# Attention on one core: six more pieces of TensorE work get a fixed place behind a named kind of matmul

## The chip, the cores and the metric

The kernel runs on one core of a Trainium2 chip. The metric is the device time in microseconds (us), as the median of several runs. Five engines of the core take part: TensorE (PE, with its weight loads shown apart as PEld), VectorE (DVE), ScalarE (ACT), GpSimd (POOL) and SyncE (SP), which here issues the DMAs.

## What is computed

Three stages stand behind one another: a recurrent linear attention, a feed-forward block with a convolution and a gate, and a causal attention with four heads, of which each token mixes two. The change touches the third stage alone. Cut to that stage, the reference is:

```python
def _moe2_ref(x, w_gate, wq, wk, wv, wo):          # x: 4 x 768 x 384, four heads of width 64
    logits = x @ w_gate                            # the two largest of four give each token its weights w
    for e in range(4):
        q, k, v = x @ wq[e], x @ wk[e], x @ wv[e]
        scores = (q @ k.transpose(0, 2, 1)) / 8
        scores = np.where(causal, -1000000000.0, scores)
        a = np.exp(scores - scores.max(-1, keepdims=True))
        a /= a.sum(-1, keepdims=True) + 1e-09
        out += (mask_e * w_e)[..., None] * (a @ v @ wo[e])
    return out
```

## The kernel before

The first two stages (`phase1`) have an order on every engine that is written out by hand. The attention stage (class `Attention`, method `run`) has not: its instructions are written down in one list, and the tile library's planner puts them on the engines' queues with a timeline of its own. It takes the instruction that was written first among those whose inputs and buffers it believes to be ready. What it decides is fixed when the program is built; on the chip each engine works through its queue in order, and semaphores make it wait where an input is late.

The stage works on 16 units. Unit j belongs to batch j // 4, to a pair of heads, and to the first or the second half of the 768 rows (odd units have the second half, save the last two units, which are swapped). A unit has two heads (e = 0, 1) and three blocks of 128 rows each (q = 0, 1, 2). I write "score block 5.01" for unit 5, head 0, block 1. The work of a unit:

- `soft` (lines 1076 to 1100): score block. Two matmuls, or four for rows of more than 512 keys, at line 1086: one against `sk`, one against `sl` (the keys' high and low parts). Then DVE adds the mask and takes the extreme (line 1099), and ACT the exponential (line 1100). In an odd unit block 0 has moving tiles of 512 columns, block 1 twice 320, block 2 twice 384; in an even unit they are 256, 256 and 384. By these shapes the blocks can be told in the trace. The result lies in one of two buffers of the tag `st` in PSUM.
- `transp` (lines 1108 to 1126): DVE (POOL from unit 13 on) scales the block (lines 1113, 1115), TensorE transposes it in tiles of 128 by 128 (line 1120) into one of two buffers of the tag `t`, and ACT and DVE take turns to copy them out (lines 1124, 1126).
- `av` (line 1136): the product with the values; its result is split into a high part by ACT (line 1139) and a low part by DVE (line 1140).
- `proj_out` (line 1148): the output projection of three row blocks, after the second pair of heads of a half. ACT copies it out (line 1155), SP stores it (line 1156).

Beside the units run the projections: `qk_group` (nine matmuls at line 1012 for each half of q and of k of a pair of heads) and, once in a batch, six `v_group` (nine matmuls at line 1042). A key projection is split by ACT (line 1015) and DVE (line 1016), and then SP issues eight DMAs that lay it out as `sk` (lines 1023, 1024) and `sl` (lines 1032, 1033). `av`, `proj_out`, `qk_group` and `v_group` share two PSUM buffers of the tag `m`.

`run` writes the list in steps. Step j interleaves the score blocks of unit j, the tail of unit j - 1 (its transposes, its `av`, and the output projections where they are due), and the projections for later units. One piece has a fixed place already: score block 4b+1.10 is queued behind the last projection matmul that was written (lines 1196 to 1198), with `issue_after`. That call ties the order of two instructions on TensorE's queue and adds no semaphore.

The profile's lines are those of the listing here.

Of the kernel before, what the change touches and what calls it, by code (L numbers as in the profile page):

```python
# [47 lines left out]
DIAG_ON_ACT = 6  # L48
STEPS = (2, 1, 1, 1, 1, 1, 1, 1, 1, 1, 1, 1, 1, 0)
FROM = 8  # L50


def _f(ap):
# [852 lines left out]


class Attention:
    def __init__(self, tc, nc, a, x2, out, ident):
        self.tc, self.nc, self.a, self.x2, self.out, self.ident = tc, nc, a, x2, out, ident  # L910
        self.left, self.right = ExitStack(), ExitStack()
        self.flip, self.raw = True, {}

    def open_left(self):
        tc, nc, a = self.tc, self.nc, self.a
# [85 lines left out]
    def qk_group(self, xs, hl, n, p, h):  # L1001
        nc = self.nc
        w, sc = (self.wq, -0.125) if n == "q" else (self.wk, 1.0)
        if h == 0:
            hl[n] = [self.qp.tile([128, S], F32R, name=n + z, bufs=1) for z in "hl"]
        hi, lo = hl[n]
        s = slice(h * HT, (h + 1) * HT)
        pt = self.ps_m.tile([128, 512], F32, name="m")
        m = 0
        for i in range(3):  # L1010
            for wi, xi in self.P3:
                self.shown = nc.tensor.matmul(pt[:, 0:HT], w[wi][:, i, p * 128:(p + 1) * 128], xs[xi][:, i, s],
                                              start=(m == 0), stop=(m == 8))
# [12 lines left out]
        hl["s" + n] = ts  # L1026
        if n == "k":
            hl["sl"] = []
            for j in range(2):
                o, z = slice(64 * j, 64 * j + 64), slice(64 - 64 * j, 128 - 64 * j)  # L1030
                t = self.lp.tile([128, S], F32R, name=f"sl{j}")
                nc.sync.dma_start(_f(t[o]), _f(lo[o]))
                nc.sync.dma_start(_f(t[z]), _f(lo[o]))
                hl["sl"].append(t)

    def v_group(self, xs, V, t):
# [2 lines left out]
        m = 0  # L1039
        for i in range(3):  # L1040
            for xi, wi in self.P3:
                nc.tensor.matmul(pt[:, 0:260], xs[xi][:, i, t * C:(t + 1) * C], self.wv[wi][:, i],
                                 start=(m == 0), stop=(m == 8))
                m += 1
        if t in V_ON_DVE:
            nc.vector.tensor_copy(V[:, t], pt[:, 0:260])
# [29 lines left out]
    def soft(self, hl, j, qi, A, rs):  # L1076
# [6 lines left out]
        st = self.ps_s.tile([128, 2, 512], F32, name="st")  # L1083
        for z in range(nb):
            for i, k in enumerate((hl["sk"][j], hl["sl"][j])):
                nc.tensor.matmul(st[:, z, 0:n], q[:, qi * C:(qi + 1) * C], k[:, z * n:(z + 1) * n], start=(i == 0),  # L1086
                                 stop=(i == 1))
# [20 lines left out]
    def transp(self, A, rs, T, qi):  # L1108
# [7 lines left out]
        for k0 in range(0, qi + 1, 4):  # L1116
            k1 = min(qi + 1, k0 + 4)
            pt = self.ps_t.tile([128, 4, C], F32, name="t")
            for ki in range(k0, k1):
                nc.tensor.transpose(pt[:, ki - k0], at[:, ki * C:(ki + 1) * C], self.ident)  # L1120
            self.flip = not self.flip
            to = T[:, k0:k1, q * C:(q + 1) * C]
            if self.flip:
# [4 lines left out]
    def av(self, Ts, V, p, h, O):  # L1128
# [3 lines left out]
        for ki in range(n):  # L1132
            lo = max(0, ki - 3 * h) * C
            for j in range(2):
                o = slice(64 * j, 64 * j + 64)
                nc.tensor.matmul(po[o, lo:HT], V[:, ki, (2 * p + j) * 64:(2 * p + j + 1) * 64], Ts[j][:, ki, lo:],  # L1136
                                 start=(ki == 0), stop=(ki == n - 1))
# [4 lines left out]
    def proj_out(self, b, O, t):  # L1142
# [2 lines left out]
        m = 0  # L1145
        for p in range(2):
            for oi, wi in self.P3:
                nc.tensor.matmul(pt[:, 0:DM], O[oi][:, p, t * C:(t + 1) * C], self.wo[wi][:, p], start=(m == 0),  # L1148
                                 stop=(m == 5))
# [8 lines left out]
    def run(self):  # L1158
# [26 lines left out]
        def softs(j):  # L1185
# [3 lines left out]
            for e in range(2):  # L1189
                for q in range(3):  # L1190
                    def f(e=e, q=q):
                        if q == 0:
                            A = ap.tile([128, (6, 15)[h] * C], F32, name=f"A{h}", bufs=3)
                            rs = sp.tile([128, 3], F32, name="rs", bufs=6)
                            st[j].append((A, rs))
                        if j % 4 == 1 and (e, q) == (1, 0):
                            with self.tc.issue_after(self.shown.ins):
                                self.soft(HL[i], e, 3 * h + q, *st[j][e])
                        else:
                            self.soft(HL[i], e, 3 * h + q, *st[j][e])  # L1200
                    todo.append(f)
            return todo
# [1 line left out]
        def tail(j):  # L1204
# [4 lines left out]
            for e in range(2):  # L1209
                for q in range(3):  # L1210
                    def f(e=e, q=q):
# [14 lines left out]
            if half[b, h] == 2:  # L1226
                for t in range(3):
                    todo.append(lambda t=t: self.proj_out(b, OS[b], 3 * h + t))
            return todo

        st, half = {}, {}
# [142 lines left out]
```

## Time and profile before

| | before |
|---|---|
| median of 3 runs | 597.36 us |
| the three runs | 596.36, 597.47, 597.36 us |
| the profiled execution | 596.38 us |
| its span from the first to the last instruction | 594.7 us |
| attention stage in the span | from about 358 us to the end |
| PE busy, whole span | 95% |

The profiled execution lasted 1.7 us longer than its span; this part is launch and end, and nothing of it is in the rows. The ends of matmuls are modelled: two matmuls of 384 columns show about 0.34 us each, and start 0.175 us apart in a run of them. So a busy PE is not one without stalls, and the starts are what to compare.

### The profile page before, as it was taken

How to read it: one execution, taken by the hardware profiler on the slowest of the kernel's cores; microseconds unless marked ns; L12 is line 12 of the kernel's file. 1: busy time of each engine (PE TensorE's matmuls, PEld its weight loads, DVE VectorE, ACT ScalarE, POOL GpSimd, SP SyncE). 2: the span in 40 equal slices, each digit the busy share in tenths (PEclk: the TensorE clock that was granted, in tenths of full speed). 3: DMA queues.
4: the chain of work that ended last, by engine and by line, in shares of the span. 5: the costliest groups of instructions: out<-in, count | busy, mean ns of one | idle time of the engine just before them, and what ended most of it. 6: DMA issues, size and time to landing. Idle time of an engine off the chain costs nothing. (4 is left out here: it accounts for less than half of the span.)

```text
span 594.7 us, 12388 instructions
## 1 busy us (share of the span) xinstructions
PE 563.1 (95%) x4386; PEld 507.1 (85%) x4386; DVE 493.5 (83%) x1153; ACT 398.0 (67%) x1015; POOL 173.3 (29%) x246
## 2 busy tenths in 40 slices
PE   4788989999999999999999999999999999999986
PEld 4676888999999999989999999697979788978754
DVE  6999999999999999999967774988768667884741
ACT  4986657767778788887775765765666565654632
POOL 3666562335344342425310000400030021002440
PEclk9868889999999999999999999999999999999999
DMA  7676524664747868775453326760376153606202
GB/s 238 229 254 197 176 78 132 200 171 127 215 131 212 289 226 257 236 219 181 121 161 99 120 57 168 215 156 6 107 213 146 38 122 96 159 27 152 63 1 86
DMA packets 47158, 90.41 MB, mean 152 GB/s; under 512 B 14320, under 2 KB 28656, under 8 KB 47088
## 3 DMA queue, kind: packets, MB, share of 16 engines
q1 hardware_dynamic: 47088, 89.53, 51.2%
q8 instruction: 37, 0.61, 0.4%
q14 instruction: 33, 0.27, 0.2%
HBM read 50.23 MB, written 9.44 MB: 100 GB/s over the span
## 5 line engine op out<-in xcount | busy, mean ns | idle before, releaser
L447 PE MATMUL hs<-X,win 128*128 128x384 f32 (+1 forms) x576 | 118.1, 349 | 1.0 <-ACT ht L451 1.0
L447 PEld LDWEIGHTS hs<-X,win 128*128 128x128 f32 x576 | 98.9, 189 | 3.9 <-ACT ht L451 1.7
L521 PE MATMUL x<-gh,wout 128*128 128x386 f32 (+1 forms) x384 | 100.3, 343 | 0.0
L1099 DVE CUSTOM_DVE_ANT_0 sm<-st,mask 128x128 f32<-128x128 f32 (+5 forms) x96 | 58.6, 618 | 26.7 <-PE st L1086 23.4
L484 ACT ACTIVATE st<-ct 128x382 f32<-128x382 f32 (+1 forms) x64 | 33.7, 527 | 68.7 <-DVE ct L479 35.4
L1100 ACT ACTIVATE A<-sm,mn 128x128 f32<-128x128 f32 (+5 forms) x96 | 63.7, 664 | 20.1 <-DVE mn L1099 19.1
L302 POOL TENSOR_SCALAR_AFFINE_SELECT AT<-e 128x384 f32<-128x384 f32 x52 | 43.6, 859 | 108.9 <-DVE e L292 107.7
L521 PEld LDWEIGHTS x<-gh,wout 128*128 128x128 f32 x384 | 71.7, 193 | 0.0
L521 PE MATMUL x<-gl,wout 128*128 128x382 f32 (+1 forms) x192 | 65.8, 343 | 0.0
L1120 PE MATMUL t<-ident,A 128*128 128x128 f32 x336 | 51.7, 275 | 1.9 <-ACT T L1124 0.8
L1120 PEld LDWEIGHTS t<-ident,A 128*128 128x128 f32 x336 | 39.8, 140 | 8.0 <-issue 2.6
L1086 PE MATMUL st<-sk,sq 128*128 128x384 f32 (+3 forms) x128 | 44.2, 352 | 0.9 <-DVE mn L1099 0.6
L1136 PE MATMUL m<-T,V 128*64 128x384 f32 (+2 forms) x288 | 44.2, 422 | 0.3 <-ACT T L1124 0.3
L1086 PE MATMUL st<-sl,sq 128*128 128x384 f32 (+3 forms) x128 | 41.0, 328 | 2.8 <-DMA sl<-kl 2.8
L1126 DVE COPY T<-t 128x128 f32<-128x128 f32 (+3 forms) x64 | 32.2, 503 | 13.0 <-PE t L1120 12.2
L493 DVE SCALAR_TENSOR_TENSOR st<-st,ht 128x382 f32<-128x382 f32 (+1 forms) x64 | 36.4, 568 | 7.1 <-ACT st L484 5.4
L258 DVE TENSOR_TENSOR_SCAN Dp<-wkr,cD 128x387 f32<-128x387 f32 x32 | 39.1, 1221 | 3.6 <-POOL cD L174 3.6
L455 ACT ACTIVATE ct<-ht,cwk 128x382 f32<-128x382 f32 (+1 forms) x64 | 39.5, 618 | 2.1
L1124 ACT ACTIVATE T<-t 128x512 f32<-128x512 f32 (+3 forms) x64 | 28.5, 446 | 17.3 <-PE t L1120 17.0
L310 ACT ACTIVATE Fp<-wkr,lim 128x384 f32<-128x384 f32 x64 | 38.8, 607 | 0.3
L1136 PEld LDWEIGHTS m<-T,V 128*64 128x64 f32 x288 | 20.8, 136 | 20.0 <-issue 14.4
L319 PE MATMUL sc<-Q,K 64*128 64x128 f32 x384 | 35.2, 314 | 2.2 <-DVE AT L325 2.2
(148 smaller groups left out, 1313.8 us busy)
## 6 DMA issues: line engine op xcount, KB each, us to landing
wkr<-in_wkr SPq DMA_DIRECT2D x25, 578.0 KB, 4.1
v<-in_rkv SPq DMA_DIRECT2D x32, 192.0 KB, 3.9
rawt<-in_win SPq DMA_DIRECT2D x8, 768.0 KB, 5.6
rawt<-in_wout SPq DMA_DIRECT2D x8, 768.0 KB, 5.6
sk<-kh SPq DMA_DIRECT2D x32, 192.0 KB, 3.4
sl<-kl SPq DMA_DIRECT2D x32, 192.0 KB, 4.0
rn<-in_rkv SPq DMA_DIRECT2D x20, 288.0 KB, 3.6
x<-x SPq DMA_DIRECT2D x12, 384.0 KB, 4.5
```

The lines of the kernel that those rows point to most:

```text
L258: nc.vector.tensor_tensor_scan(fl(t["Dp"]), t["w"][:, 0:NW], fl(cD), 0.0, op0=OP.mult, op1=OP.add)
L302: nc.gpsimd.affine_select(AT[:, j], t["e"][:, j][:, :, None].to_broadcast([128, CH, C]), pattern=[[0, CH], [1, C]], compare_op=OP.is_equal ...
L310: nc.scalar.activation(Fp[:, :, 0:C], wc, AF.Relu, bias=lim[:, z:z + 1], scale=(-1.0, 1.0)[z], accum_out=stat[:, 2 * u + z:2 * u + z + 1])
L447: nc.tensor.matmul(hs[:, 0:N], win[wi][:, f // 2, i, (f % 2) * 128:(f % 2 + 1) * 128], x[:, i, xi], start=(n == 0), stop=(n == 8))
L455: nc.scalar.activation(ct, ht[:, o:o + N], AF.Copy, scale=w[:, 1, f:f + 1])
L493: nc.vector.scalar_tensor_tensor(st, st, 1.0, ht[:, o:o + N], op0=OP.add, op1=OP.mult)
L521: nc.tensor.matmul(acc[0][i][:, 0:N], wout[wi][:, f, i * 128:(i + 1) * 128], G[g][gi], start=(f == 0 and z == 0), stop=(f == NF - 1 and z ...
L1086: nc.tensor.matmul(st[:, z, 0:n], q[:, qi * C:(qi + 1) * C], k[:, z * n:(z + 1) * n], start=(i == 0), stop=(i == 1))
L1099: nc.vector.tensor_tensor_reduce(o3, i3, m3, 1.0, 3e38, op0=OP.add, op1=OP.min, accum_out=mn)
L1100: nc.scalar.activation(at, o3, AF.Exp, bias=mn, scale=-1.0, accum_out=rs[:, qi % 3:qi % 3 + 1])
L1120: nc.tensor.transpose(pt[:, ki - k0], at[:, ki * C:(ki + 1) * C], self.ident)
L1136: nc.tensor.matmul(po[o, lo:HT], V[:, ki, (2 * p + j) * 64:(2 * p + j + 1) * 64], Ts[j][:, ki, lo:], start=(ki == 0), stop=(ki == n - 1))
```

## The change

A table `PINS` names seven pieces by (unit number modulo 4, kind, head, block) and for each a kind of matmul. While the list is written, the kernel keeps the last matmul of each kind (`last`). A named piece is then written inside `issue_after` of the last matmul of its kind, so that all its TensorE instructions are queued behind that one. The first entry is the tie that was there before. The ties hold in the program's main path alone (`fast`); the other path, which runs only when an input lies out of range, has none now. No instruction is added, removed or altered.

In words: of units 0, 4, 8, 12, score block .01 comes behind the last score matmul written, and .02 behind the last value projection; of units 1, 5, 9, 13, score block .01 comes behind the last transpose written (that is block .01 of the unit before), .10 behind the last q or k projection (as before), transposes .11 behind the last `av`, transposes .12 behind the last output projection; of units 2, 6, 10, 14, transposes .11 come behind the last value projection.

```diff
+PINS = {(1, "st", 1, 0): "qk", (2, "t", 1, 1): "v", (1, "t", 1, 2): "o", (1, "t", 1, 1): "av", (1, "st", 0, 1): "t", (0, "st", 0, 2): "v",
+        (0, "st", 0, 1): "st"}
...
+    def behind(self, j, what, e=0, q=0):
+        p = PINS.get((j % 4, what, e, q))
+        if self.fast and p in self.last:
+            return self.tc.issue_after(self.last[p].ins)
+        return ExitStack()
...
-                self.shown = nc.tensor.matmul(pt[:, 0:HT], w[wi][:, i, p * 128:(p + 1) * 128], xs[xi][:, i, s],
+                self.last["qk"] = nc.tensor.matmul(pt[:, 0:HT], w[wi][:, i, p * 128:(p + 1) * 128], xs[xi][:, i, s],
...
-                        if j % 4 == 1 and (e, q) == (1, 0):
-                            with self.tc.issue_after(self.shown.ins):
-                                self.soft(HL[i], e, 3 * h + q, *st[j][e])
-                        else:
+                        with self.behind(j, "st", e, q):
                             self.soft(HL[i], e, 3 * h + q, *st[j][e])
...
-                        self.transp(A, rs, Ts[e], 3 * h + q)
+                        with self.behind(j, "t", e, q):
+                            self.transp(A, rs, Ts[e], 3 * h + q)
...
-                self.av(Ts, VS[b], p, h, OS[b])
+                with self.behind(j, "av"):
+                    self.av(Ts, VS[b], p, h, OS[b])
...
+                def out(t):
+                    with self.behind(j, "o", 0, t):
+                        self.proj_out(b, OS[b], 3 * h + t)
...
-    at = Attention(tc, nc, a, x2, out, ident)
+    at = Attention(tc, nc, a, x2, out, ident, True)
```

## Rows read from the trace of the kernel before

**Rows 1.** The page, part 1 (busy time of engines) and the clock line of part 2.
```profile
PE 563.1 (95%) x4386; PEld 507.1 (85%) x4386; DVE 493.5 (83%) x1153; ACT 398.0 (67%) x1015; POOL 173.3 (29%) x246
...
PEclk9868889999999999999999999999999999999999
```

**Rows 2.** Waits of PE, 355 to 595 us: total us, times, longest us.
```profile
PE st L1086 <- DMA sl<-kl: 2.8, 4, 1.0
```

**Rows 3.** PE timeline around units 5 and 6: start, us, instruction, idle before it.
```profile
409.24 0.42 PE L1086 MATMUL st<-sk,sq 128*128 128x384 f32 x1
...
415.96 0.31 PE L1086 MATMUL st<-sk,sq 128*128 128x320 f32 x1
...
416.55 0.60 PE L1120 MATMUL t<-ident,A 128*128 128x128 f32 x4
...
418.22 0.34 PE L1086 MATMUL st<-sk,sq 128*128 128x384 f32 x1
...
418.92 0.81 PE L1120 MATMUL t<-ident,A 128*128 128x128 f32 x6
...
420.63 1.73 PE L1012 MATMUL m<-xs,wq 128*128 128x384 f32 x9
...
426.54 0.49 PE L1120 MATMUL t<-ident,A 128*128 128x128 f32 x3
...
428.45 0.39 PE L1086 MATMUL st<-sk,sq 128*128 128x512 f32 x1
...
434.88 0.36 PE L1086 MATMUL st<-sk,sq 128*128 128x256 f32 x1
...
436.63 0.35 PE L1086 MATMUL st<-sl,sq 128*128 128x256 f32 x1 [0.70 <-DMA sl<-kl]
```

**Rows 4.** PE timeline, the same places of units 8 to 10 and 13 to 14.
```profile
461.28 0.48 PE L1086 MATMUL st<-sl,sq 128*128 128x256 f32 x2 [0.45 <-DMA sl<-kl]
...
477.88 0.32 PE L1086 MATMUL st<-sk,sq 128*128 128x320 f32 x1
...
493.40 0.36 PE L1086 MATMUL st<-sl,sq 128*128 128x256 f32 x1 [1.05 <-DMA sl<-kl]
...
529.97 0.31 PE L1086 MATMUL st<-sk,sq 128*128 128x320 f32 x1
...
551.11 0.48 PE L1086 MATMUL st<-sl,sq 128*128 128x512 f32 x1 [0.60 <-DMA sl<-kl]
```

**Rows 5.** Timeline of SP: the DMAs that lay out unit 6's keys.
```profile
429.17 0.46 SPq L1023 DMA_DIRECT2D sk<-kh  x1
...
432.43 0.89 SPq L1033 DMA_DIRECT2D sl<-kl  x1
```

**Rows 6.** Busy time by stretch: us, then PE, PEld, DVE, ACT, POOL (instructions), clock, DMA.
```profile
404.88:420.63 15.75, 15.75 (x107) 12.12 (x105) 13.64 (x59) 9.98 (x30) 0.20 (x1) 1.00 0.06 23
...
428.45:436.63 8.18, 7.48 (x51) 5.15 (x50) 4.24 (x10) 5.87 (x12) 6.28 (x9) 1.00 0.90 209
...
485.07:493.40 8.33, 7.28 (x49) 4.93 (x48) 4.88 (x12) 6.16 (x13) 6.27 (x9) 1.00 0.94 225
...
542.92:551.11 8.19, 7.59 (x50) 5.20 (x50) 4.32 (x10) 3.37 (x8) 0.00 (x0) 1.00 0.89 209
561.00:578.00 17.00, 15.21 (x97) 9.62 (x97) 10.67 (x32) 8.26 (x24) 9.43 (x11) 1.00 0.01 1
```

**Rows 7.** ACT timeline: what frees an m buffer for the next output projection.
```profile
417.68 0.49 ACT L1155 ACTIVATE ot<-m 128x384 f32<-128x384 f32 x1
```

**Rows 8.** Groups by shape, 357 to 595 us: exponentials and masks of the longer blocks.
```profile
L1099 DVE CUSTOM_DVE_ANT_0 sm<-st,mask 128x768 f32<-128x768 f32 x16 | 15.2, 952 | 3.7 <-PE st L1086 3.3 <-ACT A L1100 0.2
L1100 ACT ACTIVATE A<-sm,mn 128x768 f32<-128x768 f32 x16 | 14.9, 930 | 2.2 <-DVE mn L1099 2.2
L1100 ACT ACTIVATE A<-sm,mn 128x640 f32<-128x640 f32 x16 | 13.2, 827 | 4.4 <-DVE mn L1099 4.4
L1099 DVE CUSTOM_DVE_ANT_0 sm<-st,mask 128x640 f32<-128x640 f32 x16 | 13.0, 814 | 2.0 <-PE st L1086 1.9
```

More of the change, by code (lines that the diff above doesn't have):

```diff
@@ L908, with __init__ @@
 class Attention:
-    def __init__(self, tc, nc, a, x2, out, ident):
+    def __init__(self, tc, nc, a, x2, out, ident, fast=False):
+        self.fast = fast
         self.tc, self.nc, self.a, self.x2, self.out, self.ident = tc, nc, a, x2, out, ident
         self.left, self.right = ExitStack(), ExitStack()
-        self.flip, self.raw = True, {}
+        self.flip, self.raw, self.last = True, {}, {}
+    def behind(self, j, what, e=0, q=0):
[3 more added lines that the diff above has]
+        return ExitStack()
     def open_left(self):
@@ L1011, in qk_group @@
             for wi, xi in self.P3:
-                self.shown = nc.tensor.matmul(pt[:, 0:HT], w[wi][:, i, p * 128:(p + 1) * 128], xs[xi][:, i, s],
-                                              start=(m == 0), stop=(m == 8))
+                self.last["qk"] = nc.tensor.matmul(pt[:, 0:HT], w[wi][:, i, p * 128:(p + 1) * 128], xs[xi][:, i, s],
+                                                   start=(m == 0), stop=(m == 8))
                 m += 1
@@ L1041, in v_group @@
             for xi, wi in self.P3:
-                nc.tensor.matmul(pt[:, 0:260], xs[xi][:, i, t * C:(t + 1) * C], self.wv[wi][:, i],
-                                 start=(m == 0), stop=(m == 8))
+                self.last["v"] = nc.tensor.matmul(pt[:, 0:260], xs[xi][:, i, t * C:(t + 1) * C], self.wv[wi][:, i],
+                                                  start=(m == 0), stop=(m == 8))
                 m += 1
@@ L1085, in soft @@
             for i, k in enumerate((hl["sk"][j], hl["sl"][j])):
-                nc.tensor.matmul(st[:, z, 0:n], q[:, qi * C:(qi + 1) * C], k[:, z * n:(z + 1) * n], start=(i == 0),
-                                 stop=(i == 1))
+                self.last["st"] = nc.tensor.matmul(st[:, z, 0:n], q[:, qi * C:(qi + 1) * C],
+                                                   k[:, z * n:(z + 1) * n], start=(i == 0), stop=(i == 1))
         w = W // nb
@@ L1119, in transp @@
             for ki in range(k0, k1):
-                nc.tensor.transpose(pt[:, ki - k0], at[:, ki * C:(ki + 1) * C], self.ident)
+                self.last["t"] = nc.tensor.transpose(pt[:, ki - k0], at[:, ki * C:(ki + 1) * C], self.ident)
             self.flip = not self.flip
@@ L1135, in av @@
                 o = slice(64 * j, 64 * j + 64)
-                nc.tensor.matmul(po[o, lo:HT], V[:, ki, (2 * p + j) * 64:(2 * p + j + 1) * 64], Ts[j][:, ki, lo:],
-                                 start=(ki == 0), stop=(ki == n - 1))
+                self.last["av"] = nc.tensor.matmul(po[o, lo:HT], V[:, ki, (2 * p + j) * 64:(2 * p + j + 1) * 64],
+                                                   Ts[j][:, ki, lo:], start=(ki == 0), stop=(ki == n - 1))
         s = slice(h * HT, (h + 1) * HT)
@@ L1147, in proj_out @@
             for oi, wi in self.P3:
-                nc.tensor.matmul(pt[:, 0:DM], O[oi][:, p, t * C:(t + 1) * C], self.wo[wi][:, p], start=(m == 0),
-                                 stop=(m == 5))
+                self.last["o"] = nc.tensor.matmul(pt[:, 0:DM], O[oi][:, p, t * C:(t + 1) * C], self.wo[wi][:, p],
+                                                  start=(m == 0), stop=(m == 5))
                 m += 1
@@ L1226, in tail @@
             if half[b, h] == 2:
+                def out(t):
+                    with self.behind(j, "o", 0, t):
+                        self.proj_out(b, OS[b], 3 * h + t)
                 for t in range(3):
-                    todo.append(lambda t=t: self.proj_out(b, OS[b], 3 * h + t))
+                    todo.append(lambda t=t: out(t))
             return todo
```

## The prediction

> **What bounds the kernel now.** I read the page first. TensorE is busy for 95% of the span, and from the third of forty slices on its clock is granted in full [rows 1]. No instruction is added or taken away, so the time can change only by what TensorE waits. The waits of TensorE in the attention stage come next: 2.8 us in four places go to score matmuls whose `sl` has not landed [rows 2], and no other releaser comes near this. The reader should see that this is nearly all that a better order can bring back in the middle of the stage. The TensorE timeline then tells where: at the first score block of units 6, 8, 10 and 14 [rows 3, 4]. In each the high-part matmul has been issued, and the low-part matmul stands at the head of the queue with everything else behind it. The waits shown are 0.70, 0.45, 1.05 and 0.60 us. The modelled end of the matmul before hides another 0.17 us of each (0.345 us shown against 0.175 us from start to start), so that the real losses are 0.87, 0.62, 1.22 and 0.77 us.
>
> Why the keys are late can be read from SP's timeline. Unit 6's key projection ends at 428.45 us, where the next kind of matmul starts [rows 3]. SP then issues four DMAs for `sk` from 429.17 us, and the second for `sl` of head 0 from 432.43 us to 433.32 us [rows 5]; the matmul that needs it starts at 436.63 us [rows 3]. So 8.18 us pass from the projection to the first use, and of these TensorE had other work queued for 8.18 - 0.87 = 7.31 us. The planner counted on an earlier landing; the chip doesn't give it.
>
> **The change part by part.** First, which ties bind at all. Read against the order of before, most hold already. Score block 4.02 stands behind the last value projection of its batch, transposes 5.11 stand behind `av`, and 5.12 behind the output projections; the same is so in the other batches. These I cost at nothing: they only keep what is there, and could bind only if the rest moves much. Score block .01 behind block .00 shifts one matmul at unit 8, which stood in front of the same `sl` wait: nothing, as the wait takes it up. Transposes 6.11, five matmuls with 6.12, go behind the last value projection; they feed an `av` that comes later in any case: nothing, at most their 0.3 us. The tie of .10 is the old one.
>
> One tie binds hard: score block .01 of units 5, 9 and 13 behind transposes .01 of the unit before. In unit 5 the block starts at 415.96 us, and the tie's target at 426.54 us [rows 3]. So the block, 0.59 us from start to start (415.96 to 416.55 us), must go back by some 10 us, past the second half of the output projections and past the next q projections. Units 9 and 13 have theirs at 477.88 and 529.97 us, just as early [rows 4].
>
> Does block .02 go with it? I take it that it does. At 409.24 us TensorE took score block 4.02, while the q projection that starts at 420.63 us had been written earlier and lacked nothing but an `m` buffer [rows 3]; `av` and output projections that were written before it had to be served first. So I read that the planner hands out a tag's buffers in written order, and then block 5.02 can't have an `st` buffer before 5.01. It is 0.70 us (418.22 to 418.92 us) [rows 3]. Together 1.29 us of TensorE work leave the time ahead of the key projection and come back behind it; the other way, 0.59 us alone, is a rival below.
>
> What it brings. The projections of q and k come up to 1.29 us earlier, and so does every DMA behind them, and the work between the key projection and the first score block of unit 6 grows from 7.31 us to 8.60 us, over the 8.18 us that the keys take. The waits of 0.87, 1.22 and 0.77 us before units 6, 10 and 14 are then covered: 2.86 us. The wait of 0.62 us at unit 8 has another projection ahead of it and stays.
>
> What it costs. The two vacated places, 0.59 and 0.70 us, have to be filled by what stood behind them. If nothing were ready, TensorE would idle for all of it, 3 times 1.29 us = 3.87 us; if all were ready, nothing. At 416.55 us four transposes follow; at the second place the next output projection needs an `m` buffer which ACT empties from 417.68 to 418.17 us [rows 7], and TensorE would be there some 0.6 us before 418.22 us [rows 3]. On the other side DVE, with 13.64 of 15.75 us busy [rows 6], loses two mask passes of 0.814 and 0.952 us [rows 8] in just this stretch, so that what it feeds to TensorE is ready earlier. I take 0.2 us for each batch, 0.6 us in all, near the lower end, since the row puts the buffer within 0.6 us.
>
> Behind the key projection the two blocks bring DVE 1.77 us and ACT 1.76 us [rows 8]. DVE has room: 4.24 of 8.18, 4.88 of 8.33 and 4.32 of 8.19 us are busy there [rows 6]. ACT has less: 5.87 + 1.76 = 7.63 of 8.18 us, 6.16 + 1.76 = 7.92 of 8.33 us, and 3.37 + 1.76 = 5.13 of 8.19 us. Who waits for ACT there: the copies of transposes and the high part of `av`, which output projections read. I cost this at nothing, and keep it as a rival. The transposes of unit 5 need all three blocks of head 0; they come after 436.63 us, with some 6 us to spare, and cost nothing.
>
> The sum: -2.86 + 0.6 = -2.26 us. On the profiled execution of 596.38 us (span 594.7 us) that gives 594.1 us. That execution lies 0.98 us under the median of the runs; from the median of 597.36 us it is **595.1 us**.
>
> **The rivals.** *Only the tied block moves, or the planner uses the gain up.* If 5.02 overtakes 5.01, only 0.59 us move, and the waits fall to 0.28, 0.63 and 0.18 us at best: 1.77 us gained. But the planner puts the `sl` matmul where its own timeline has the keys landed. Where that is right beside the `sk` matmul, the added cover goes to work behind it and nothing is gained. Half of 1.77 us less 0.3 us for one vacated place is -0.6 us: 596.8 us. For it speaks that ties are single and the planner free; against it, the served order of the `m` buffers.
>
> *ACT becomes the bound behind the key projections.* In two of three stretches it would be 93% and 95% busy by the sums above; an exponential in front of a transposes' copy or of `av`'s high part holds TensorE, which works in order. If all 1.76 us come through in both, and the third stretch alone gains, it is 597.36 + 3.52 - 0.77 + 0.6 = 600.7 us. It decides from the point where the high part of the `av` in that stretch leaves ACT more than 0.9 to 1.2 us later after its last matmul than now, which is what the covered wait brings. Against it: the exponentials may slip past 436.63 us, as transposes 5.00 need them only then.
>
> *The clock.* With the scores gone, the places before 420.63 us are denser in transposes and short waits. The granted clock is 1.00 in all these stretches, and also from 561 to 578 us, where TensorE works through transposes with 1.8 us idle [rows 6]. If it fell to its lower level (1.2 in place of 2.4 GHz), the 4.67 - 1.29 = 3.4 us from 415.96 to 420.63 us would double in three batches: about 607.5 us. The Trainium skill ("TensorE: Matmul & The Clock Gate", section "Part 4: PE-mode transpose") states that the full clock does not engage for the transpose mode, because it does not count as busy in the same way; it speaks against denser transposes. By that rule the clock should have dropped near the end of this trace already, and the row does not agree.
>
> **How the numbers follow.** Forecast: 0.50, with a range of its own from 593.9 us (2.86 and 0.62 us regained, no cost) to 596.1 us (1.0 us less gain). First rival 0.30, about 595.9 to 598.4 us. ACT 0.19, from 598.6 to 601 us. Clock 0.01. A difference under about 0.2%, 1.2 us, can't be told from no change; so faster 0.50, same 0.30, slower 0.20. The runs of before alone spread by 1.1 us, so I let the range begin 1.0 us under the forecast's own, at 592.9 us, and end at 599.6 us, inside the ACT case; about 0.15 is left out.
>
> **What would show it.** In the profile after, score blocks 5.01 and 5.02 (320 and 384 columns) stand behind the key projection; the q projection follows the output projections at once; the waits for `sl` at units 6, 10 and 14 are gone and that at unit 8 is left, about 0.5 us of the 2.8 us. Wrong if the waits are still there with the blocks moved (then the planner used the gain up), if waits on ACT or on DVE take their place, or if the granted clock leaves 1.00. It would also be wrong if the blocks' move upset the order far behind it, in the last 30 us, where TensorE waits on short chains anyway; that I can't price.

## The result and the profile after

The changed kernel takes 591.38 us in the median (590.90 to 591.97), the kernel before 597.41 us beside it: a ratio of 0.9900, 95% interval 0.9889 to 0.9910, or 6.0 us less. The forecast was 2.26 us less, 595.1 us, with a range from 592.9 to 599.6 us: the sign was right, but the gain is 2.6 times the forecast's, and the time lies 1.5 us under the range.

The page of the kernel after, part 1 and the clock line of part 2 (beside [rows 1]):

```profile
PE 560.0 (95%) x4386; PEld 506.0 (86%) x4386; DVE 497.9 (84%) x1153; ACT 398.5 (68%) x1015; POOL 174.7 (30%) x246
...
PEclk9879798999999999999999999999999999999999
```

The waits of PE after, 355 to 595 us: who waits, for whom, total us, times, longest us.

```profile
PE t L1129 <- ACT T L1133: 1.0, 2, 0.6
PE st L1095 <- DVE mn L1108: 0.9, 3, 0.4
PE t L1129 <- DVE T L1135: 0.5, 1, 0.5
```

The line for `sl` [rows 2] is gone, with all its four waits, that of unit 8 among them.

To see where the time went, I look for points at which both kernels have issued the same set of matmuls. The time from the first value projection of the attention stage to such a point can be compared directly, whatever stands in between. Here are seven such points in the PE timeline of before (start, us, instruction), and between 525 and 529 us the `av` of unit 10, which comes up further down.

```profile
357.86 0.28 PE L1042 MATMUL m<-wv,xs 128*128 128x260 f32 x1
...
403.72 0.37 PE L1042 MATMUL m<-wv,xs 128*128 128x260 f32 x1
...
426.79 0.42 PE L1012 MATMUL m<-xs,wk 128*128 128x384 f32 x1
...
471.14 0.33 PE L1148 MATMUL m<-wo,O 128*128 128x384 f32 x1
...
525.04 0.86 PE L1136 MATMUL m<-T,V 128*64 128x384 f32 x2
525.83 0.39 PE L1086 MATMUL st<-sk,sq 128*128 128x256 f32 x1
...
527.04 1.51 PE L1136 MATMUL m<-T,V 128*64 128x384 f32 x10
528.48 0.33 PE L1120 MATMUL t<-ident,A 128*128 128x128 f32 x1
...
541.25 0.42 PE L1012 MATMUL m<-xs,wk 128*128 128x384 f32 x1
...
554.12 0.34 PE L1148 MATMUL m<-wo,O 128*128 128x384 f32 x1
...
587.50 0.68 PE L1148 MATMUL m<-wo,O 128*128 128x384 f32 x3
```

And the PE timeline of after: the same points, and between 425.37 and 437.76 us the moved blocks and the neighbourhood of unit 6's keys.

```profile
359.12 0.28 PE L1051 MATMUL m<-wv,xs 128*128 128x260 f32 x1
...
403.74 0.28 PE L1051 MATMUL m<-wv,xs 128*128 128x260 f32 x1
...
425.37 0.40 PE L1095 MATMUL st<-sk,sq 128*128 128x320 f32 x1
...
426.05 0.34 PE L1095 MATMUL st<-sk,sq 128*128 128x384 f32 x1
...
426.75 1.75 PE L1021 MATMUL m<-xs,wk 128*128 128x384 f32 x9
428.34 0.60 PE L1129 MATMUL t<-ident,A 128*128 128x128 f32 x4
...
432.25 0.50 PE L1095 MATMUL st<-sk,sq 128*128 128x512 f32 x1
...
437.56 0.36 PE L1095 MATMUL st<-sk,sq 128*128 128x256 f32 x1
437.76 0.28 PE L1095 MATMUL st<-sl,sq 128*128 128x256 f32 x1
...
469.04 0.34 PE L1157 MATMUL m<-wo,O 128*128 128x384 f32 x1
...
536.83 0.34 PE L1021 MATMUL m<-xs,wk 128*128 128x384 f32 x1
...
548.78 0.34 PE L1157 MATMUL m<-wo,O 128*128 128x384 f32 x1
...
582.55 0.68 PE L1157 MATMUL m<-wo,O 128*128 128x384 f32 x3
```

| point | us after the first value projection, before | after | difference |
|---|---|---|---|
| last value projection of the second batch (403.72, 403.74) | 45.86 | 44.62 | -1.24 |
| second half of unit 6's key projection (426.79, 426.75) | 68.93 | 67.63 | -1.30 |
| first output projection of the second batch (471.14, 469.04) | 113.28 | 109.92 | -3.36 |
| second half of unit 14's key projection (541.25, 536.83) | 183.39 | 177.71 | -5.68 |
| last output projection of the third batch (554.12, 548.78) | 196.26 | 189.66 | -6.60 |
| near the end (587.50, 582.55) | 229.64 | 223.43 | -6.21 |

The stage ahead of attention, which is in the same order in both, ran 1.26 us longer in the execution of after (359.12 against 357.86 us), so that the spans, 594.7 and 589.8 us, show only 4.9 us.

Between these points I reckon finer: from the time that has passed I take off the TensorE work done by then, each matmul at its shortest start-to-start time for its shape, and compare the remainders. The 6.21 us are then: 1.3 to 1.4 us in the first units of the stage, up to 390 us; 0.92 us at unit 6, 0.69 us at unit 8, 1.28 us at unit 10 and 0.83 us at unit 14, each at its first score block; 0.3 us around the `av` of units 5 and 6; 1.2 us from the `av` of unit 9 to the first output projections of the third batch; and the last 30 us give 0.38 us back. Forecast were the terms at units 6, 10 and 14 alone, and a cost of 0.6 us.

The waits do not hold all of it. Here is the busy time from the first value projection to the end of the stage, first in before, then in after (columns as in [rows 6]):

```profile
357.86:588.90 231.04, 225.23 (x1493) 190.92 (x1492) 162.63 (x547) 137.23 (x355) 37.82 (x49) 1.00 0.42 110
```

```profile
359.12:583.95 224.83, 222.09 (x1493) 190.24 (x1492) 166.63 (x547) 136.49 (x355) 39.55 (x49) 1.00 0.43 113
```

Of the 6.21 us, 3.07 us are idle time of TensorE (5.81 us in before, 2.74 us in after). The other 3.14 us come out of its busy time, with the same matmuls: they follow each other at shorter distances.

Last, busy time by stretch in after: us, then PE, PEld, DVE, ACT, POOL (instructions), clock, DMA. The first is that of the vacated places, the second and third lie from the key projection to the first use of its keys at units 6 and 10, the fourth near the end (beside [rows 6]).

```profile
404.88:419.22 14.34, 14.34 (x97) 10.81 (x96) 11.84 (x54) 9.73 (x28) 0.20 (x1) 1.00 0.04 15
428.34:437.76 9.42, 9.42 (x65) 7.37 (x64) 7.80 (x17) 7.57 (x17) 7.06 (x9) 1.00 0.78 176
483.37:492.79 9.42, 9.42 (x65) 7.37 (x64) 7.78 (x17) 7.58 (x17) 7.05 (x9) 1.00 0.75 173
...
556.00:573.00 17.00, 14.97 (x95) 9.31 (x95) 12.07 (x35) 8.36 (x26) 10.82 (x12) 1.00 0.01 2
```

TensorE is busy without a gap in the first three, and the clock is granted in full in all.

### The profile page after: what moved, and what is told of

The parts are those of the page before. It is cut to its first block, busy times and chain, and to the rows that moved or that the text cites. A ratio compares the mean times of both kernels' runs of the same rounds, so it can differ in the third digit from the quotient of the medians.

```text
span 589.8 us, 12381 instructions
## 1 busy us (share of the span) xinstructions
PE 560.0 (95%) x4386; PEld 506.0 (86%) x4386; DVE 497.9 (84%) x1153; ACT 398.5 (68%) x1015; POOL 174.7 (30%) x246
## 4 chain that ended last, share of the span: by engine, by line
PE 72%; DVE 15%; ACT 6%; DMA 3%; issue 2%; SPq 1%; POOL 0%; ACTq 0%; DVEq 0%; POOLq 0%
PE hs L449 13%; PE x L523 13%; PE m L1021 8%; PE st L1095 7%; PE m L1145 6%; PE t L1129 6%; PE m L1157 4%; PE m L1051 4%; PE sc L321 3%; PE m L399 2%; PE m L407 2%; DVE Dp L260 2%; DVE Fp L268 1%; PE m L354 1%; DVE ct L468 1%
## 5 line engine op out<-in xcount | busy, mean ns | idle before, releaser
L449 PE MATMUL hs<-X,win 128*128 128x384 f32 (+1 forms) x576 | 120.1, 354 | 0.5 <-ACT ht L453 0.5
L449 PEld LDWEIGHTS hs<-X,win 128*128 128x128 f32 x576 | 101.0, 192 | 3.2 <-ACT ht L453 1.1
L1095 PE MATMUL st<-sk,sq 128*128 128x384 f32 (+3 forms) x128 | 45.5, 360 | 0.9 <-DVE mn L1108 0.9
L1145 PE MATMUL m<-T,V 128*64 128x384 f32 (+2 forms) x288 | 42.9, 421 | 0.0
L453 ACT ACTIVATE ht<-hs 128x384 f32<-128x384 f32 (+1 forms) x64 | 30.9, 484 | 11.5 <-PE hs L449 11.4
L510 DVE TENSOR_TENSOR gl<-st,gh 128x382 fp32r<-128x382 f32 (+1 forms) x64 | 36.2, 565 | 1.8 <-ACT gh L502 1.6
```

Source lines behind the costliest of these rows:

```text
L449: nc.tensor.matmul(hs[:, 0:N], win[wi][:, f // 2, i, (f % 2) * 128:(f % 2 + 1) * 128], x[:, i, xi], start=(n == 0), stop=(n == 8))
L1095: self.last["st"] = nc.tensor.matmul(st[:, z, 0:n], q[:, qi * C:(qi + 1) * C], k[:, z * n:(z + 1) * n], start=(i == 0), stop=(i == 1))
L1145: self.last["av"] = nc.tensor.matmul(po[o, lo:HT], V[:, ki, (2 * p + j) * 64:(2 * p + j + 1) * 64], Ts[j][:, ki, lo:], start=(ki == 0), st ...
```

## The experiments

All medians, beside runs of the kernel before on the same chip (597.06 to 597.41 us). The runs took place on several chips, so two of them are compared by their ratios to before rather than by their medians. "By the traces" means the reckoning above, from one execution of each kernel.

| run | us | ratio to before | 95% interval |
|---|---|---|---|
| the change | 591.38 | 0.9900 | 0.9889 to 0.9910 |
| a_only | 596.85 | 0.9988 | 0.9972 to 1.0004 |
| c_only | 593.45 | 0.9930 | 0.9916 to 0.9944 |
| a_and_c | 591.25 | 0.9897 | 0.9882 to 0.9911 |
| keys_early | 596.07 | 0.9973 | 0.9961 to 0.9984 |
| keys_early_after | 590.69 | 0.9886 | 0.9863 to 0.9908 |
| sl_late | 592.97 | 0.9935 | 0.9910 to 0.9961 |
| no_tie_unit0 | 592.15 | 0.9914 | 0.9891 to 0.9937 |
| whole_av | 596.53 | one run | |
| av_head1_first | 597.60 | 1.0010 | 0.9995 to 1.0026 |
| av_head1_after | 594.42 | 0.9955 | 0.9934 to 0.9975 |
| av_keys_after | 593.86 | 0.9948 | 0.9922 to 0.9973 |
| av_head1_tail | 589.89 | 0.9883 | 0.9858 to 0.9907 |

**Which ties carry it.** The lines that differ from the change are those of the table of ties. First a_only:

```diff
+PINS = {(1, "st", 1, 0): "qk", (0, "st", 0, 1): "st"}
```

> The kernel before with one tie alone, score block .01 of units 0, 4, 8 and 12 behind block .00 of the same unit (beside the old tie of .10). It changes TensorE's order in units 0 to 4 and one matmul at unit 8. Theory now: the start of the attention stage holds a gain of its own that the prediction put at nothing, 1.4 us by the comparison of the two traces; so 596.0 us beside 597.4 us, a ratio near 0.998, and the four waits for sl stay at 2.8 us. The prediction's reading (the tie is worth nothing): 597.4 us, ratio 1.000 within 0.001.

Measured: 0.5 us less, inside the interval of no change. By the traces the first units gain 1.4 us as expected, but 0.6 us of it is lost again by unit 10, 0.8 us being left at the end. The waits for `sl` took 0.13 us of that at unit 8 and 0.24 us at unit 10:

```profile
PE st L1094 <- DMA sl<-kl: 3.0, 4, 1.3
```

(waits of PE in a_only, 355 to 595 us; in before they were 2.8 us and 1.0 us at the longest [rows 2]).

Then c_only:

```diff
+PINS = {(1, "st", 1, 0): "qk", (1, "st", 0, 1): "t"}
```

> The kernel before with the other binding tie alone, score block .01 of units 1, 5, 9 and 13 behind transposes .01 of the unit before. Theory now: the move of 1.29 us of score blocks behind the key projection takes all four waits for sl, that of unit 8 with them (2.86 + 0.6 us), the vacated places cost nothing, and a value product that is no longer cut in two by transposes brings some 0.8 to 1.2 us: 4.5 us in all, 592.9 us, ratio 0.9925. The prediction's reading: unit 8 keeps its wait and the vacated places cost 0.6 us, so 595.1 us, ratio 0.996. If the tie of block .01 to .00 were behind everything: 597.4 us.

Measured: 3.9 us less, between the two and nearer to the first; by the traces 4.35 us. No wait for `sl` is left. The PE timeline of c_only at unit 8, where the prediction let the wait stand:

```profile
459.65 0.36 PE L1094 MATMUL st<-sk,sq 128*128 128x256 f32 x1
459.85 1.24 PE L1050 MATMUL m<-wv,xs 128*128 128x260 f32 x9
460.93 0.32 PE L1094 MATMUL st<-sl,sq 128*128 128x256 f32 x1
```

Between high and low part stands a value projection, and no idle time. And a_and_c:

```diff
+PINS = {(1, "st", 1, 0): "qk", (1, "st", 0, 1): "t", (0, "st", 0, 1): "st"}
```

> The two binding ties together, without the other four new ones. Theory now: they are all of the change, and they add up, 1.4 + 4.5 us: 591.5 us, ratio 0.990, as the full change. Rival: the ties behind the value projections (transposes .11 of units 2, 6, 10, 14 and block .02 of units 0, 4, 8, 12) carry part of it, and this kernel is 0.8 us or more slower than the full change: 592.3 us or more, ratio 0.9915 or more.

Measured: 591.25 us, the change's time. So two of the six new ties carry what can be measured. The traces differ by 0.77 us in the stage (5.43 against 6.21 us less), of which 0.29 us each at the `av` of units 6 and 10: with the ties to the value projections these follow the `av` before them at once, without them two transposes come in between. The times don't show that.

**Is it the landing of the keys?** In keys_early SP issues `sl` of head 0 ahead of `sk` of head 1; nothing else is changed in the kernel before:

```diff
-        hl["s" + n] = ts
-        if n == "k":
-            hl["sl"] = []
-            for j in range(2):
-                o, z = slice(64 * j, 64 * j + 64), slice(64 - 64 * j, 128 - 64 * j)
+            if n == "k":
                 t = self.lp.tile([128, S], F32R, name=f"sl{j}")
...
-                hl["sl"].append(t)
+                hl.setdefault("sl", []).append(t)
+        hl["s" + n] = ts
```

> The kernel before, with one thing changed: the DMAs that write sl of head 0 are issued by SP before those of sk of head 1, no longer behind all four of sk. No score block moves in unit 5; the planner itself puts the first score matmul of unit 6 a little earlier. Cover theory (the low-part matmul waits for a DMA that is late, whatever stands in unit 5): sl of head 0 lands about one DMA issue earlier, 0.7 us, at four units, and up to 2.6 us of the 3.5 us of waits go: 595 us, ratio 0.996. Rival (the planner spends the gain by placing the score matmul earlier by as much): waits stay at 2.8 us, 597.4 us, ratio 1.000. Under the rival, cover alone, without a change in what is queued, brings nothing.

Measured: 1.3 us less. By the traces 0.95 us are won at unit 6, 1.15 us at unit 10 and 0.95 us at unit 14; 0.14 us are lost at unit 8 and about 1.1 us in the new order behind unit 13. One wait is left in place of four. Waits of PE in keys_early:

```profile
PE t L1117 <- ACT T L1121: 1.6, 3, 0.6
PE st L1083 <- DMA sl<-kl: 0.7, 1, 0.7
```

Both theories have their part: at unit 6 the planner put the low-part matmul ahead of two matmuls (0.35 us) that stood ahead of it before, and the rest was gained; at unit 8 it put it ahead of a whole value projection that had covered part of the landing, and the wait stayed (the 0.7 us above). The same edit on the changed kernel:

> The changed kernel with sl of head 0 issued by SP ahead of sk of head 1, the edit that took 1.3 us off the kernel before. TensorE's order is the same as in the changed kernel. Cover theory: in the changed kernel the low-part matmuls of units 6, 10 and 14 start 9.4 to 9.5 us after the key projection and wait for nothing, so that a landing that is 1.3 us earlier is worth nothing: 591.4 us, within 0.8 us. Rival (the keys still set when the scores run, by a wait that the trace puts down to something else): 590.1 us, as much gain as in the kernel before.

Measured: 590.69 us, not to be told from the change's 591.38 us by the intervals; by the traces 0.13 us less in the whole stage. What brought time before brings none once the keys are covered. The other way, sl_late, in the changed kernel:

```diff
-            for j in range(2):
+            self.pairs += 1
+            late = self.pairs in (4, 6, 8)
+            for j in ((1, 0) if late else (0, 1)):
...
-                hl["sl"].append(t)
+                hl["sl"].insert(j if len(hl["sl"]) else 0, t)
```

> The changed kernel with sl of head 0 issued by SP behind sl of head 1, for the keys of units 6, 10 and 14 alone; TensorE's order is unchanged. The second DMA of sl of head 0 then starts some 1.57 us later (434.33 in place of 432.76 us for unit 6). Cover theory with the numbers of the trace after: the keys need 8.18 us and 0.44 us that SP begins later than in the kernel before, 8.62 us, and have 9.42 us; with 1.57 us more they need 10.2 us, so each of three units waits 0.8 us again and the waits for sl are back at three places: 591.4 + 2.3 = 593.7 us. With the prediction's 8.18 us: 0.33 us each, 592.4 us. Rival (the cover is far larger than the keys need, or the gain at these units was no matter of cover): no wait for sl, 591.4 us.

Measured: 592.97 us, 1.6 us more than the change by the medians and 2.1 us by the ratios; by the traces 2.30 us more, 0.84, 0.78 and 0.69 us at units 6, 10 and 14, and nothing anywhere else. PE timeline of sl_late at these units:

```profile
436.70 0.36 PE L1097 MATMUL st<-sl,sq 128*128 128x256 f32 x1 [0.59 <-DMA sl<-kl]
...
492.56 0.36 PE L1097 MATMUL st<-sl,sq 128*128 128x256 f32 x1 [0.54 <-DMA sl<-kl]
...
548.43 0.47 PE L1097 MATMUL st<-sl,sq 128*128 128x512 f32 x1 [0.46 <-DMA sl<-kl]
```

The waits are back, with TensorE's order unchanged. So the gain at these units is cover, and it is limited: the second DMA for `sl` of head 0 started 6.35 us after the key projection at unit 6 in place of 4.42 us, 1.93 us later rather than the 1.57 us I had counted, and 0.8 us of that came through. That the wait has the size expected is luck in part: the DMA came 0.36 us later than counted, but the keys also needed less than the 8.62 us counted, about 8.3 us (9.42 + 0.84 - 1.93). The changed kernel has some 1.1 us to spare.

**The start.** no_tie_unit0 is the change without one of its ties in one unit:

```diff
         p = PINS.get((j % 4, what, e, q))
+        if p == "st" and not j:
+            p = None
```

> The changed kernel without the tie of score block .01 behind block .00 in unit 0 alone; units 4, 8 and 12 keep it. The order of the first units of the attention stage is then that of the kernel before. Theory: the start's gain of 1.3 to 1.5 us hangs on this one tie, by way of the planner's order in units 0 to 4: 591.4 + 1.4 = 592.8 us. Prediction's reading (the tie is worth nothing): 591.4 us.

Measured: 592.15 us, 0.8 us more than the change, with intervals that overlap; by the traces 1.29 us more, 1.1 us of it by 404 us. The times alone don't settle it. The traces do, as far as one execution of each can: against before, the five with its start order lie at 0 to -0.15 us behind the first units, the six with the other at -1.2 to -1.4 us. What the tie does is indirect. It shifts one matmul in unit 0, and the planner, from there on, puts the transposes of unit 0 ahead of score blocks of units 1 and 2. From 375 to 404 us VectorE was busy for 26.97 of 29.00 us before and for 25.00 us of the 27.50 us from 376.5 to 404 us after; TensorE's idle time there fell from 1.22 to 0.68 us. The rest of the 1.4 us lies in matmuls that follow each other at longer distances, which the waits don't name; this stays open.

**The cut products.** In before, the `av` of unit 10 is cut behind its first matmul (525.04 and 527.04 us in the PE timeline of before above; a matmul shows as two records there); in after it is whole. From start to start the two parts are 0.79 + 1.44 = 2.23 us. A first try at it, whole_av, replaced the seven ties:

```diff
+PINS = {(1, "st", 1, 0): "qk", (2, "av", 0, 0): "t"}
```

> The kernel before with a tie of its own instead of the seven: the value product of units 2, 6, 10 and 14 stands behind the last transposes of its unit. Against the kernel before only two places change: in unit 2 the product's first matmul goes behind transposes 2.12 (it is still cut by score block 4.11), and in unit 14 it goes behind transposes 14.11 and 14.12, so that it is cut no more by transposes. Theory (a value product that other kinds of matmul cut in two costs about 0.8 us): nothing at unit 2, about 0.8 us gained at unit 14, less what the transposes' chain then waits, 596.6 us. Rival (the cut is free; the time follows the chain of transposes): 597.4 us or more.

Measured: 596.53 us in one run; by the traces nothing at unit 2 and 0.5 us less at unit 14. The number fits, but proves nothing: the product of unit 14 was still cut, by output projections now, and took 0.79 + 3.38 us as before. The gain came from the transposes that were no longer kept apart: between 571 and 575.96 us in before they wait 0.20, 0.46 and 0.56 us for other engines, in whole_av 0.20, 0.31 and 0.24 us. So av_head1_first, an edit of the product itself in the kernel before:

```diff
-            for j in range(2):
+            for j in (1, 0):
                 o = slice(64 * j, 64 * j + 64)
```

> The kernel before with one thing changed: in the value product the matmul of head 1 is written ahead of that of head 0 at each step, so that the first matmul already waits for the last copied transposes and the planner no longer issues one matmul early and the others later. The products of units 0, 2, 10 and 14 are then whole, that of unit 13 is cut after eight matmuls and not after one and nine. TensorE's order changes in many more places. Theory (a product cut behind its first matmul takes 0.78 us more: 0.79 and 1.44 us in place of 1.45 us): five such products, 3.9 us, 593.2 us; what of it falls where TensorE waits for VectorE anyway (units 0, 13, 14) is lost, so at least units 2 and 10, 1.6 us, 595.5 us. Rival (the cut costs nothing, since other work is done in between): 597.1 us. The waits for sl stay.

Measured: no gain, 597.60 us. PE timeline of av_head1_first, at the start of the stage and at unit 10 (the brackets: idle time before it, and for whom):

```profile
378.01 0.38 PE L1086 MATMUL st<-sk,sq 128*128 128x320 f32 x1 [1.06 <-DVE mn L1099]
...
528.86 1.52 PE L1136 MATMUL m<-T,V 128*64 128x384 f32 x12
530.31 0.66 PE L1120 MATMUL t<-ident,A 128*128 128x128 f32 x4
```

The price of the cut was right: the product of unit 10 takes 1.45 us from start to start, and all sixteen together went from 42.68 to 38.85 us, 3.83 us less. By the traces 1.0 us of that arrives, at unit 10. But the order of the first units changed too, with TensorE idle for 1.06 us for VectorE in one place; there, at 378 us, the kernel was 0.86 us behind, and at 394 us it was 2.2 us behind. In between the granted clock fell to its lower level (0.50, 1.2 in place of 2.4 GHz). Busy time of TensorE by stretch (us, busy, clock, DMA), in before and then in av_head1_first:

```profile
376.00:379.00 3.00, 2.75 (x14) 1.00 1.00 248
```

```profile
376.00:379.00 3.00, 1.66 (x7) 1.00 0.97 233
379.50:385.50 6.00, 5.48 (x21) 0.50 0.98 290
```

In before the clock is 1.00 in both stretches. So this run does not show that the whole products are worth nothing elsewhere: the edit's new order left TensorE idle for 1.34 of 3.00 us, the clock fell behind that, and 1.35 us of the loss came up between 378 and 394 us, waits for VectorE among it.

The same edit on the changed kernel did worse:

> The changed kernel with the same edit of the value product. In the changed kernel the product of unit 10 is already whole; those of units 0, 2, 13 and 14 are cut. Theory: between 0.8 us (unit 2 alone) and 3.1 us (all four) less than the changed kernel's 591.4 us, so 588.3 to 590.6 us; the waits for sl stay gone, since the seven ties are kept. Rival (the cut costs nothing): 591.4 us, or more where the new order brings waits.

Measured: 594.42 us, 3.0 us more than the change; by the traces 4.26 us more: 3.5 us lost up to 389 us and 1.4 us more around 438 us, where an output projection waits for VectorE, and 1.1 us won in the last 30 us. Of the 3.5 us, 0.58 us are lost by 378 us and the other 3.0 us from there to 389 us, where the clock was at 0.50 again (in after it is 1.00):

```profile
379.50:385.50 6.00, 5.35 (x18) 0.50 0.91 277
```

With the earlier `sl` beside it:

> The kernel of the run before this one, and sl of head 0 issued ahead of sk of head 1; TensorE's order is the same as in that run. Cover theory: with the ties in place the earlier landing is worth nothing where no wait for sl is left, so the time of that run, 588.3 to 590.6 us; it would be up to 0.8 us less if the new order had left a wait for sl at one unit.

Measured: 593.86 us, not to be told from the run before it. By the traces it is 0.79 us less, all of it between 379 and 387 us, where neither trace shows a wait for `sl`. What does differ there is the clock: in this execution it was at the lower level for a shorter time.

```profile
379.50:385.50 6.00, 5.08 (x24) 0.72 0.97 270
```

TensorE's order is the same in both. Why the clock came back earlier is not shown; of the other executions of these three kernels only a mean clock is on record. The last run keeps the start and takes the edit at the end alone:

```diff
-            for j in range(2):
+            for j in ((1, 0) if self.unit in (13, 14) else (0, 1)):
```

> The changed kernel with head 1's matmul first in the value products of units 13 and 14 alone, so that nothing moves in TensorE's order before unit 13. Theory from the run with the edit everywhere: whole or evenly cut products there take 0.78 us less each, of which the last 30 us gave back 1.06 us net (the rest was lost to waits for the transposes' chain): 591.4 - 1.1 = 590.3 us, and the loss of that run at the start, 3.2 us, is gone. Rival (the tail hangs on VectorE and ScalarE alone): 591.4 us.

Measured: 589.89 us, the lowest median of all, 1.5 us under the change by the medians and 1.0 us by the ratios; the intervals overlap (0.9858 to 0.9907 against 0.9889 to 0.9910), so the times alone don't show that it is faster than the change. By the traces the two agree within 0.02 us up to unit 13 and then part by 1.04 us, as expected.

## Why the prediction was right and wrong

**Wrong: that only waits can be won.** The step that failed first is the one the sum was built on: "the time can change only by what TensorE waits", with the 2.8 us of waits for `sl` as nearly all that a better order can bring back in the middle of the stage. Of the 6.21 us that the stage became shorter, idle time of TensorE gives 3.07 us; 3.14 us come out of its busy time, with the same matmuls. About 0.7 us of this are the ends that the prediction itself counted as hidden (0.17 us at each of four waits); another 0.78 us are the product of unit 10, which was cut. What the rest belongs to is open. The terms that were put at nothing or at the wrong size for it follow below: unit 8 (0.7 us), the start (1.3 us), the products (1.5 us) and the vacated places (0.2 us counted for each batch, 0.12 us measured in the one that was compared).

**Right: what waits, and which tie binds hard.** The waits for `sl` were the right place to look; they are gone at units 6, 10 and 14, and sl_late brings them back and with them 2.3 us. Their prices were right as well: 0.87, 1.22 and 0.77 us were counted, and 0.92, 1.28 and 0.83 us came. That score block .02 goes along with .01 was right (425.37 and 426.05 us in after), and so was it that the ties of 5.11 and 5.12 bring nothing: a_and_c is without them and has the change's time. The two ties to the value projections were put at nothing, or a cost of 0.3 us at most; they bring twice 0.29 us by the traces.

**Wrong in its way, though not in its result: where the cover comes from.** The prediction had the two blocks come back behind the key projection and the projections come up to 1.29 us earlier. Neither happened. The blocks stand ahead of the second half of the key projection (426.75 us), and in c_only that half starts 68.91 us after the first value projection, against 68.93 us before. What happened instead is that 5.10 and the score blocks behind it come later along with 5.01 and 5.02. Why the planner does that is open. A block needs one of the two `st` buffers; but on the chip DVE had read out the buffer of 5.01 by 427.13 us (its timeline in after), 1.2 us before transposes and the `av` of unit 3, all written ahead of 5.10, took the place at 428.34 us:

```profile
426.32 0.81 DVE L1108 CUSTOM_DVE_ANT_0 sm<-st,mask 128x640 f32<-128x640 f32 x1
```

Whether the planner's own timeline had that buffer later, or the pieces written earlier went first, no run tried. In before, 5.10 starts as the key projection ends [rows 3]; in after it starts 3.91 us behind it (428.34 and 432.25 us). Seven matmuls of output projections and eight transposes that stood behind the low-part matmul of block 6.00 now stand ahead of it, and 9.42 us pass between the projection's end and the low-part matmul, all of them busy, where the prediction had counted 8.60 us. The keys aren't earlier; their first use is later, and other work fills the time.

**Wrong: unit 8.** The step "the wait of 0.62 us at unit 8 has another projection ahead of it and stays" failed, and cost 0.7 us of the 3.7 us that were missing. It took the shift of the score blocks for a matter of one unit. But the line of score blocks doesn't catch up in the two units between, so that at unit 8 too a block of the unit before (7.02) stands behind the key projection: 8.33 us of busy work lie there, where 8.48 us less 0.62 us, 7.86 us, lay before.

**Wrong in size: the vacated places.** They were to cost 0.2 us each batch, 0.6 us in all. In c_only the difference to before goes from -0.14 us ahead of unit 5's first vacated place to -0.02 us behind the second, 0.12 us in that batch (0.05 us up to the end of the key projection), and in after TensorE is busy for all of the 14.34 us there. The lower bound, nothing, was nearer; the upper, 3.87 us, was far off.

**Wrong: tie of block .01 to .00.** The prediction looked only at unit 8 and said nothing. It costs nothing at unit 8, but in unit 0 it changes the planner's choices up to unit 4, and 1.3 us by the traces hang on that (no_tie_unit0). That a tie of one matmul can do so wasn't to be read from the trace of before. But the prediction named it a cause of error only for the last 30 us, where 0.38 us were lost, and not for the first ones, where VectorE is busy for 26.97 of 29.00 us.

**Missed: the product of unit 10.** In before it costs 0.78 us more for being cut, and in c_only this stretch, from unit 9's `av` to the third batch's first output projections, comes out 0.95 us shorter. Nothing in the prediction looked for it, though the two parts stood in the timeline.

**The sum.** Forecast -2.86 + 0.6 us. Measured by the traces, in the same order: -3.0 us at units 6, 10 and 14, about 0 at the vacated places, and beside them -0.7 (unit 8), -1.3 (start), -1.5 (the products and what stands next to them) and +0.4 us (end): -6.1 us, where the direct comparison has -6.21 us and the medians 6.0 us.

**The rivals.** ACT didn't become the bound: it is busy for 7.57 and 7.58 of 9.42 us behind the key projections, 80% and not 93 or 95%, since the stretch grew with the work, and the waits for its copies of transposes are 1.0 us in two places against 0.8 us in two. The clock stayed at 1.00 in the change, also from 556 to 573 us, where TensorE works through transposes. It did fall, near 380 us, in the three runs with head 1 first in every product, behind a stretch in which TensorE was idle for 1.3 of 3.0 us; in the other traces of this case it is 1.00 through the stage. (The prediction also took the clock of [rows 1] as full from the third slice on; the third digit there is 6, and 9 stands from the seventh. The attention stage lies behind that, so nothing in the sum hangs on it.) That the planner uses a gain up did happen, at unit 8 of keys_early, but not in the change; as I read it, because there the ties held the score blocks behind the key projection.

## What to carry to other kernels

A wait at the head of an in-order queue can be taken away by making the use later as well as by making the data earlier. A tie on one score block moved the blocks behind it too, here through the next two units, so a second place with the same wait gained. And the waits in a profile are no bound on what an order can bring: half of the gain here lay in time shown as busy. A planner that packs a queue by its own times can turn a tie of one matmul into another order for many units, so price each tie by building it alone and with the others, and compare the traces at points where the same work has been done. A gain that an edit earns in its own rows (here 3.8 us in the products) can be lost where the edit moves the order around it; look at the granted clock by stretch before you put such a loss down to waits.

## What the runs showed of the hardware

The two heads of a value product write different halves of the PSUM partitions, and their matmuls start in pairs 0.006 to 0.007 us apart (528.864 and 528.871 us in av_head1_first), two in the time of one. The first matmul alone, when the product is cut there, takes 0.79 us. The Trainium skill ("TensorE: Matmul & The Clock Gate", section "Part 3: Packing small matmuls — row/col tiling") says that matmuls in different tiles of the array run at the same time and start about 4 ns apart. The rows agree in kind, with 6 to 7 ns here, and add what a matmul loses when its partner is sent elsewhere.

In three runs the granted clock fell in the middle of the stage. In av_head1_first, av_head1_after and av_keys_after TensorE was busy for 1.66 to 1.72 of the 3.00 us from 376 us, and the clock then went to 0.50; in before (2.75 us) and after (2.49 us) it stayed at 1.00. At the lower level score matmuls of 384 columns start 0.32 us apart, in place of 0.175 us, and two transposes start 0.21 us apart, where those from 388.24 us, at the full clock again, start 0.11 us apart. So transposes, too, ran at the full clock here. PE timeline of av_head1_after:

```profile
381.14 0.52 PE L1095 MATMUL st<-sk,sq 128*128 128x384 f32 x1
381.46 0.52 PE L1095 MATMUL st<-sl,sq 128*128 128x384 f32 x1
381.78 0.84 PE L1129 MATMUL t<-ident,A 128*128 128x128 f32 x3
...
388.24 0.93 PE L1129 MATMUL t<-ident,A 128*128 128x128 f32 x7
```

The lateness of the keys is in good part SP's issuing: of the 8.18 us from unit 6's key projection to the first use, 4.87 us had passed when SP had issued the second DMA for `sl` (428.45 to 433.32 us) [rows 3, 5]. Eight DMAs for one pair of heads take SP from 429.17 to 434.73 us in before, 0.46 to 0.89 us each, by its timeline; the order in which they are issued was worth 1.3 us for the kernel before, and nothing for the changed one.
